# Folding the last three pieces of the first transform stage to sum and difference, with its stores on another queue and one weight load moved back

## The chip, the cores and the metric

The kernel runs on one core of one Trainium2 chip. The metric is the device time of one execution in microseconds, as the median of several runs; lower is better. The engines named below are TensorE (PE in the profile), VectorE (DVE), ScalarE (ACT), GpSimd (POOL) and SyncE (SP). SP only issues DMA transfers here; ACT and POOL can issue them as well.

## The reference, cut to what matters

```python
X = np.fft.fft(x, axis=1)          # x: (8, 3136, 256) float32
X = np.fft.fft(X, axis=2)
x = X.real
mu, var = mean and variance of x over the last axis
xn = (x - mu) / np.sqrt(var + 1e-06) * g_ln
return x + np.maximum(xn @ w_ch1, 0.0) @ w_ch2     # w_ch1: 256x1024, w_ch2: 1024x256
```

A real part of a two-dimensional FFT for each of eight batches, then a layer norm and a two-layer MLP with a residual.

## The kernel before, in words

The transform along the sequence (3136 = 64 x 49) goes in two steps. **Step 1** is a 64-point transform for each of 49 residues; it is done in seven *pieces* (`i` = 0..6), each with its own load of 512 KB (`load_x(b, i)`, tile `xs`). Its result goes through `store1` to a DRAM scratch and comes back in another layout through `relayout` (tile `s2`). **Step 2** (`step2`) sums over the 49 residues, and its PSUM result is split into a high and a low part (`ckh`, `ckl`) that the MLP's matmuls read. The main loop then runs the MLP (`moe1_a`, `moe1_b`, `moe2`) over chunks of 256 rows, with the later batches' steps 1 and 2 placed between its matmuls.

Before the loop stands a head, written out by hand, of some 40 us. It does three things at once: step 1 of batch 0 from the seven loads of `x`; the conversion of the first weight matrix, given as float64, to two fp32 parts; and the same for the second matrix. The first matrix comes in four quarters of 512 KB (`load_w1(0..3)`, called w1_0 to w1_3 here). For each quarter ACT computes `ew` (`convert_z`), and DVE the rest: `mw` and `fw` (`convert_m`), two operations on `ew` (`convert_b`) and the scaled quarter `gw` (`finish_w1`). PE then multiplies two quarters at a time with a table (`transform_w1`, tile `psw`), ACT rounds the result (`round_w1`, `w_hi`), and a remainder is formed (`rest_w1`, `w_lo`). The second matrix's first two quarters (`load_w2(0)`, `load_w2(1)`, called w2_0 and w2_1) are loaded into the places of w1_0 and w1_1, so each waits until those have been read.

In step 1 the channels are folded first: `fold_zw` makes two 256-column tiles z and w of a piece. For batch 0, PE then forms the sum part and the difference part by accumulating in PSUM: four fp32 matmuls of 256 columns per piece, z and w with one table for the sum half, z and w with the table and its negative for the other half. The later batches form the sum and the difference on POOL (`fold_eo`) and use split operands. Two channels (0 and 128) go apart, through `ends` on POOL and `step1_ends` on PE and ACT.

The order on PE, ACT, DVE and POOL is the order in which the program is written (`manual_schedule`), as is SP's in the head. DMAs that SP and ACT issue take eight completion semaphores in turn, `DMAHW0` to `DMAHW7`; one that reuses a semaphore first waits, on its issuing engine, until the transfer that had it before has landed.

The lines that matter in the profile of before: L255 and L257 are step 1's matmuls, L265 the copy of a piece out of PSUM, L269 `store1`, L276 `relayout`, L309 step 2's matmuls, L330 and L334 `ckh` and `ckl`, L520 to L535 and L563 the conversion on DVE, L528 its ACT part, L549 and L554 the weight loads, L573 `transform_w1`, L679 `warm_up` (bf16 matmuls on zeros between the weight transforms and step 2).

Of the kernel before, what the change touches and what calls it, by code (L numbers as in the profile page):

```python
# [25 lines left out]
ALU = mybir.AluOpType  # L26
# [120 lines left out]
def tile_kernel(ctx: ExitStack, tc: tile.TileContext, x, g_ln, w1, w2, tu, tab, tz, ty, tw, out):  # L147
    nc = tc.nc
# [30 lines left out]
    def load_x(b, i):  # L179
        in_order(nc.sync.dma_start(xs[:, i], x[b, i]))  # L180
# [26 lines left out]
        eng.tensor_tensor(out=z, in0=a[:, :, 1:129], in1=c[:, :, 255:127:-1], op=ALU.add)  # L207
        eng.tensor_tensor(out=w, in0=a[:, :, 255:127:-1], in1=c[:, :, 1:129], op=ALU.add)

    def fold_eo(b, i):  # L210
        z, w = zw.pop((b, i))
        f = work.tile([128, 2, 2, 128], F32, tag="fold", name=f"f{b}_{i}")
        nc.gpsimd.tensor_tensor(out=f[:, :, 0], in0=z, in1=w, op=ALU.add)
        nc.gpsimd.tensor_tensor(out=f[:, :, 1], in0=z, in1=w, op=ALU.subtract)
        pieces[b, i] = [f]

    def fold_hi(b, i):
# [29 lines left out]
    def step1(b, i):  # L247
        alloc1(b)
        ps = psum.tile([128, 2, 2, 128], F32, tag="y" if b else f"acc{i % 2}", name=f"ps1_{b}_{i}",
                       bufs=1 if b else 2)  # L250
        if b == 0:
            z, w = zw.pop((b, i))
            for h in range(2):
                o = ps[:, :, h]
                nc.tensor.matmul(o, tu_s[:, 0:128], z, start=(h == 0), stop=False,  # L255
                                 skip_group_check=True)
                nc.tensor.matmul(o, tu_s[:, 128 * h:128 * h + 128], w, start=False, stop=True,  # L257
                                 skip_group_check=True)
        else:
            p = pieces.pop((b, i))  # L260
            for n, (ti, xi) in enumerate(PASSES):
                nc.tensor.matmul(ps, (t1_hi, t1_lo)[ti], p[xi],  # L262
                                 start=(n == 0), stop=(n == 2))
        s = s1[b][:, 2 * i:2 * i + 2]
        nc.scalar.copy(s[:, :, :, :127], ps[:, :, :, :127])  # L265
# [13 lines left out]
    gb = group_bounds()  # L279
# [266 lines left out]
    def load_w1(n):  # L546
        wp = w1p_all[:, 4 * n:4 * n + 4].rearrange("p a d -> p (a d)").bitcast(I64)
        i, k = n % 2, n // 2
        nc.sync.dma_start(wp, w1[128 * i:128 * i + 128, 512 * k:512 * k + 512])  # L549
        w1p.append(wp)  # L550

    def load_w2(n):
        wp = w1p[n]
        nc.sync.dma_start(wp.rearrange("p (f d) -> p f d", f=2), w2v[:, 2 * n:2 * n + 2])  # L554
        w2p.append(wp)
# [126 lines left out]
    with tc.manual_schedule(engines={E.PE, E.Activation, E.DVE, E.Pool}):  # L682
        with tc.manual_schedule(engines={E.SP}):
            nc.vector.memset(one, 1.0)
            for t in (warm, warm_h):
                nc.vector.memset(t, 0.0)
            for n, t in ((3, warm), (5, warm_h)):
                warm_up(n, t)
            nc.scalar.dma_start(g_s, g_ln.rearrange("(i p) -> p i", p=128))
            nc.scalar.activation(one, one, AF.Sqrt)  # L690
            nc.sync.dma_start(tu_s, tu)
            load_x(0, 0)
            load_x(0, 1)
            load_w1(0)
            for i in (2, 3, 4):
                load_x(0, i)
            load_w1(1)
            for i in (5, 6):
                load_x(0, i)
            load_w1(2)  # L700
            load_w1(3)
            nc.sync.dma_start(tw_all, tw)
            nc.gpsimd.memset(zmu, 0.0)
            nc.gpsimd.memset(masked, 0.0)
            ends(0, 0, 6)
            fold_zw(0, 0, nc.vector)
            step1(0, 0)
            nc.vector.tensor_scalar_mul(g_s, g_s, 2.0 ** -20)
            fold_zw(0, 1, nc.vector)
            convert_z("w1_0", w1p[0])  # L710
            step1(0, 1)
            convert_m("w1_0", w1p[0])
            fold_zw(0, 2, nc.vector)
            step1(0, 2)
            convert_b("w1_0")
            load_w2(0)
            nc.sync.dma_start(tab_s[:, :, :gb[4]], tab[:, :, :gb[4]])
            nc.sync.dma_start(tz_s, tz)
            step1_ends(0, 0, 6)
            for i in range(3):  # L720
                store1(0, i, nc.scalar if i % 2 else nc.gpsimd)
            ends(0, 6, 10)
            fold_zw(0, 3, nc.vector)
            step1(0, 3)
            convert_z("w1_1", w1p[1])
            fold_zw(0, 4, nc.vector)
            step1(0, 4)
            finish_w1(0)
            step1_ends(0, 6, 10)
            store1(0, 3, nc.scalar)  # L730
            store1(0, 4, nc.gpsimd)
            ends(0, 10, NS)
            convert_m("w1_1", w1p[1])
            fold_zw(0, 5, nc.vector)
            step1(0, 5)
            convert_z("w1_2", w1p[2])
            convert_b("w1_1")
            load_w2(1)
            fold_zw(0, 6, nc.vector)
            step1_ends(0, 10, NS)  # L740
            store1(0, 5, nc.scalar)
            step1(0, 6)
            store1(0, 6, nc.gpsimd)
            finish_w1(1)
            convert_z("w1_3", w1p[3])
            convert_m("w1_2", w1p[2])
            convert_b("w1_2")
            finish_w1(2)
            relayout(0, 0, 4)
            relayout(0, 4, 8)  # L750
            load_w2(2)
            nc.sync.dma_start(tab_s[:, :, gb[4]:gb[8]], tab[:, :, gb[4]:gb[8]])
            relayout(0, 8, 16)
            nc.scalar.copy(minus, tw_all[:, 512:])
            transform_w1(0, 0)
            transform_w1(0, 1)
            round_w1(0)
            convert_m("w1_3", w1p[3])
            convert_b("w1_3")
            load_w2(3)  # L760
            nc.sync.dma_start(ty_s, ty)
            nc.sync.dma_start(tab_s[:, :, gb[8]:], tab[:, :, gb[8]:])
            for i in range(NU):
                load_x(1, i)
            finish_w1(3)
            transform_w1(1, 0)
            rest_w1(0)
            convert_z("w2_0", w2p[0])
            convert_z("w2_1", w2p[1])
            rest_w1_copy(0)  # L770
            transform_w1(1, 1)
            round_w1(1)
            convert_m("w2_0", w2p[0])
            convert_b("w2_0")
            f = finish_w2(0)
            split_w2(0, f)
            convert_m("w2_1", w2p[1])
            convert_b("w2_1")
            warm_up(15, warm_h)
            step2(0, "m")  # L780
            step2(0, "hl")
            step2(1, "m")
            step2(1, "hl", 0)
            f = finish_w2(1)
            moe1_a(0, ((1, 0), (0, 0), (0, 1)))
            split_w2(1, f)
            step2(0, "f")
            moe1_a(1, ((1, 0), (0, 0), (0, 1)))
            rest_w1(1)
            moe1_b(0)  # L790
            moe1_a(2)
            moe1_b(1)
            moe1_b(2)
            moe1_a(3)
            rest_w1_copy(1)
            step2(1, "f")
            convert_a("w2_2", w2p[2])
            step2(1, "hl", 1)
            moe2(0)
            moe1_b(3)  # L800
            moe1_a(4)
            convert_b("w2_2")
            f = finish_w2(2)
            nc.gpsimd.tensor_scalar(out=neg, in0=ty_s[:, 1, 129:130], scalar1=2.0, scalar2=-1.0,
                                    op0=ALU.mult, op1=ALU.add)
            moe2(1)
            step2(2, "m")
            moe1_b(4)
            split_w2(2, f)
            moe1_a(5)  # L810
            step2(2, "hf")
            step2(2, "l")
            convert_a("w2_3", w2p[3])
            moe2(2)
            add_late(6, convert_b, "w2_3")
            add_late(6, lambda: w2f.append(finish_w2(3)))
            add_late(7, lambda: split_w2(3, w2f.pop()))
            add_late(14, split, t1_hi, t1_lo, tu_s[:, 0:128])

        main.append(True)  # L820
        lag, last = 3, 8 * NCH
        for s in range(6, last):
            moe1_b(s - 1)
            moe1_a(s)
            for fn, args in late.get(s, ()):
                fn(*args)
            moe2(s - lag)
            for fn, args in after.get(s, ()):
                fn(*args)
        moe1_b(last - 1)  # L830
        inverse_std(LC)
        moe2(last - 3)
        for i, side in ((0, 0), (1, 0), (0, 1), (1, 1)):
            for t in (last - 2, last - 1):
                moe2(t, ((i, side),))
            finish_last(i, side)
# [18 lines left out]
```

## Time and profile before

| | |
|---|---|
| median of 3 runs | 999.56 us (999.49 to 1001.34) |
| profiled execution, its own time | 1001.5 us |
| its span, first to last instruction | 999.7 us |
| PE busy | 988.3 us (99%) |
| DVE, ACT, POOL busy | 817.8, 534.8, 248.3 us |
| granted TensorE clock | 1.000 |

The profiled execution took 1.8 us more than its span. PE is busy nearly all the time; the one place where it is not is the head, where the first of the page's forty slices (25 us each) shows DVE at 6 tenths and POOL at 1. All that the change touches lies in the first 37 us.

### The profile page before, as it was taken

The page shows a single profiled execution, that of the slowest core. Times are in us where ns is not written, and L with a number is a line of the kernel's source. Part 1 is how long each engine was busy: PE and PEld are TensorE (multiplying, and loading weights), DVE is VectorE, ACT ScalarE, POOL GpSimd, SP SyncE. Part 2 cuts the span into 40 slices and gives each one's busy share as a digit, 9 for nine tenths or more (in the row PEclk, how much of TensorE's full clock was granted, in tenths as well). Part 3 has the DMA queues.
Part 4 walks back from the last instruction along what each step waited for, and adds up shares of the span by engine and source line. Part 5 has one row for each costly group of instructions (what it writes and reads, how often), then busy time and mean ns, then how long its engine had stood idle before and what let it go on. Part 6 is the DMA issues. An engine that isn't in the chain of part 4 may idle for free.

```text
span 999.7 us, 21759 instructions
## 1 busy us (share of the span) xinstructions
PE 988.3 (99%) x8288; PEld 966.4 (97%) x8289; DVE 817.8 (82%) x2190; ACT 534.8 (53%) x1416; POOL 248.3 (25%) x278
## 2 busy tenths in 40 slices
PE   9999999999999999999999999999999999999998
PEld 6799999999999999999999999999999999999998
DVE  6788878788888888888887888888888888787887
ACT  3555555555555555555555556555555555554553
POOL 1145434212411432232342124113322300000000
PEclk9999999999999999999999999999999999999999
DMA  9943352124222242121521242212310112100101
GB/s 342 264 151 113 121 159 85 64 75 132 91 73 76 75 133 99 66 75 64 170 85 54 85 134 89 95 54 71 111 53 35 54 52 87 43 23 22 44 22 43
DMA packets 41528, 92.10 MB, mean 92 GB/s; under 512 B 4176, under 2 KB 18704, under 8 KB 40528
## 3 DMA queue, kind: packets, MB, share of 16 engines
q1 hardware_dynamic: 40016, 88.87, 27.1%
q8 instruction: 66, 1.08, 0.5%
q0 software_dynamic: 320, 1.05, 0.3%
q10 hardware_dynamic: 1088, 0.79, 0.2%
q14 instruction: 38, 0.31, 0.1%
HBM read 50.32 MB, written 40.37 MB: 91 GB/s over the span
## 4 chain that ended last, share of the span: by engine, by line
PE 88%; DVE 7%; ACT 2%; DMA 1%; issue 1%; ACTq 0%; SPq 0%; DVEq 0%
PE acc L404 49%; PE ab L354 24%; PE ps L309 5%; PE psy L428 4%; PE ps L262 3%; DVE h_lo L369 2%; DVE h L360 1%; DVE h L361 1%; ACT h_hi L368 1%; PE pw L679 1%; PE ps L255 1%; DMA scratch<-s 1%; PE ps L257 1%; DMA s<-scratch 1%; DVE st L450 0%
## 5 line engine op out<-in xcount | busy, mean ns | idle before, releaser
L404 PE MATMUL acc<-w_hi,h_lo 128*128 128x256 f32 x1568 | 435.2, 278 | 0.2 <-DVE h_lo L369 0.2
L404 PE MATMUL acc<-w_lo,h_hi 128*128 128x256 f32 x1568 | 435.0, 277 | 0.0
L404 PE MATMUL acc<-w_hi,h_hi 128*128 128x256 f32 x1568 | 435.0, 277 | 0.0
L369 DVE SCALAR_TENSOR_TENSOR h_lo<-h,h_hi 128x512 fp32r<-128x512 f32 x392 | 295.5, 754 | 148.7 <-ACT h_hi L368 146.6
L368 ACT ACTIVATE h_hi<-h 128x512 fp32r<-128x512 f32 x392 | 249.9, 638 | 296.6 <-DVE h L361 296.4
L404 PEld LDWEIGHTS acc<-w_hi,h_hi 128*128 128x128 f32 x1568 | 295.6, 189 | 0.0
L404 PEld LDWEIGHTS acc<-w_hi,h_lo 128*128 128x128 f32 x1568 | 294.6, 188 | 0.5 <-DVE h_lo L369 0.4
L404 PEld LDWEIGHTS acc<-w_lo,h_hi 128*128 128x128 f32 x1568 | 294.7, 188 | 0.0
L354 PE MATMUL ab<-ckl,w_hi 128*128 128x256 f32 x768 | 218.8, 285 | 2.2 <-DVE h L361 2.1
L354 PE MATMUL ab<-ckh,w_lo 128*128 128x256 f32 x768 | 213.6, 278 | 0.5 <-ACT ckh L330 0.3
L354 PE MATMUL ab<-ckh,w_hi 128*128 128x256 f32 x768 | 213.1, 277 | 0.0
L225 POOL TENSOR_TENSOR fl<-f,fh 128x512 fp32r<-128x512 f32 x49 | 64.0, 1307 | 513.1 <-ACT fh L219 475.7
L360 DVE TENSOR_TENSOR h<-asb,ab 128x256 f32<-128x256 f32 x384 | 158.7, 413 | 1.6 <-ACT asb L359 1.5
L361 DVE TENSOR_TENSOR h<-asb,ab 128x256 f32<-128x256 f32 x384 | 158.9, 414 | 0.0
L354 PEld LDWEIGHTS ab<-ckl,w_hi 128*128 128x128 f32 x768 | 144.3, 188 | 5.9 <-issue 1.7
L354 PEld LDWEIGHTS ab<-ckh,w_lo 128*128 128x128 f32 x768 | 144.4, 188 | 3.1 <-ACT ckh L330 0.5
L354 PEld LDWEIGHTS ab<-ckh,w_hi 128*128 128x128 f32 x768 | 144.8, 189 | 0.0
L359 ACT COPY asb<-ab 128x256 f32<-128x256 f32 x384 | 138.1, 360 | 11.6 <-PE ab L354 9.7
L265 ACT COPY s<-ps 128x508 f32<-128x508 f32 x56 | 32.7, 584 | 67.0 <-PE ps L262 53.3
L309 PE MATMUL ps<-tab_s,s 112*128 112x98 f32 (+1 forms) x512 | 65.5, 273 | 1.1 <-DMA s<-scratch 1.1
L309 PEld LDWEIGHTS ps<-tab_s,s 112*128 112x128 f32 x512 | 61.8, 191 | 1.6 <-issue 1.6
L330 ACT CAST ckh<-ps 128x392 fp32r<-128x392 f32 (+49 forms) x112 | 39.8, 356 | 43.0 <-PE ps L309 42.8
(108 smaller groups left out, 965.5 us busy)
## 6 DMA issues: line engine op xcount, KB each, us to landing
xs<-x SPq DMA_DIRECT2D x56, 512.0 KB, 3.9
out<-o SPq DMA_DIRECT2D x96, 256.0 KB, 2.0
scratch<-s SPq DMA_DIRECT2D x49, 256.0 KB, 2.3
s<-scratch SPq DMA_DIRECT2D x7, 1792.0 KB, 10.0
w1p_all<-w SPq DMA_DIRECT2D x8, 512.0 KB, 8.6
scratch<-s POOLq DMA_DIRECT2D x4, 256.0 KB, 6.0
s<-scratch SPq DMA_DIRECT2D x2, 448.0 KB, 5.9
s<-scratch SPq DMA_DIRECT2D x1, 896.0 KB, 12.1
```

Source lines behind the costliest of these rows:

```text
L225: nc.gpsimd.tensor_tensor(out=lo, in0=f, in1=hi.bitcast(F32), op=ALU.subtract)
L265: nc.scalar.copy(s[:, :, :, :127], ps[:, :, :, :127])
L309: nc.tensor.matmul(ps[:, h, k0 - base:k1 - base], s2[b][:KP, g, 128 * h:128 * h + 128], tab_s[:, h, k0:k1], start=(h == 0 and g == 2 * j), ...
L330: nc.scalar.copy(hi, src)
L354: nc.tensor.matmul(pt, wt[wi][:, j, fs], ch[xi][:, j, :w], start=(n == 0), stop=(n == 2))
L359: nc.scalar.copy(asb[:, :w], pa)
L360: nc.vector.tensor_tensor(out=h[:, :w], in0=asb[:, :w], in1=pb, op=ALU.add)
L361: nc.vector.tensor_tensor(out=h[:, w:], in0=asb[:, :m], in1=pb[:, :m], op=ALU.subtract)
L368: nc.scalar.activation(h_hi, h, AF.Relu)
L369: nc.vector.scalar_tensor_tensor(out=h_lo, in0=h, scalar=0.0, in1=h_hi.bitcast(F32), op0=ALU.max, op1=ALU.subtract)
L404: nc.tensor.matmul(acc[c, i][:, side], hs[xi][:, h0:h0 + 128], ws[wi][:, f], start=(f == 0 and side == 0 and n == 0), stop=(f == 7 and n = ...
L428: nc.tensor.matmul(ps[:, j, :129 + j], ck[:, j], ty_s[:, j, :129 + j], start=(j == 0), stop=True, skip_group_check=True)
```

## The change: what it does

For pieces 4, 5 and 6 of batch 0, the sum and the difference are made ahead of PE by `fold_eo`, for piece 4 on POOL and for pieces 5 and 6 on DVE, into one tile of 512 columns, and PE does one fp32 matmul of 512 columns with the table in place of four of 256. All seven stores of batch 0 go through ACT's queue; before, four of them (pieces 0, 2, 4, 6) were issued by POOL. The load of w1_1 moves behind the seven loads of `x`, and the table `tw` ahead of w1_2. The conversion of w1_0 is finished later, and all of the conversions of w1_1, w1_2 and w1_3 stand behind the last store. The load of w2_1 moves behind the first `relayout`, and the first part of the table `tab` and `tz` behind the last store.

```diff
-    def fold_eo(b, i):
+    def fold_eo(b, i, eng=nc.gpsimd):
         z, w = zw.pop((b, i))
         f = work.tile([128, 2, 2, 128], F32, tag="fold", name=f"f{b}_{i}")
-        nc.gpsimd.tensor_tensor(out=f[:, :, 0], in0=z, in1=w, op=ALU.add)
-        nc.gpsimd.tensor_tensor(out=f[:, :, 1], in0=z, in1=w, op=ALU.subtract)
+        eng.tensor_tensor(out=f[:, :, 0], in0=z, in1=w, op=ALU.add)
+        eng.tensor_tensor(out=f[:, :, 1], in0=z, in1=w, op=ALU.subtract)
...
-        if b == 0:
+        if (b, i) in zw:
             z, w = zw.pop((b, i))
...
+        elif b == 0:
+            nc.tensor.matmul(ps, tu_s[:, 0:128], pieces.pop((b, i))[0], start=True, stop=True)
...
             for i in (2, 3, 4):
                 load_x(0, i)
-            load_w1(1)
             for i in (5, 6):
                 load_x(0, i)
+            load_w1(1)
+            nc.sync.dma_start(tw_all, tw)
             load_w1(2)
             load_w1(3)
-            nc.sync.dma_start(tw_all, tw)
...
             for i in range(3):
-                store1(0, i, nc.scalar if i % 2 else nc.gpsimd)
+                store1(0, i, nc.scalar)
...
             fold_zw(0, 5, nc.vector)
+            fold_eo(0, 5, nc.vector)
             step1(0, 5)
-            convert_z("w1_2", w1p[2])
-            convert_b("w1_1")
-            load_w2(1)
             fold_zw(0, 6, nc.vector)
+            fold_eo(0, 6, nc.vector)
             step1_ends(0, 10, NS)
             store1(0, 5, nc.scalar)
             step1(0, 6)
-            store1(0, 6, nc.gpsimd)
+            store1(0, 6, nc.scalar)
+            finish_w1(0)
+            nc.sync.dma_start(tab_s[:, :, :gb[4]], tab[:, :, :gb[4]])
+            nc.sync.dma_start(tz_s, tz)
+            convert_z("w1_1", w1p[1])
+            convert_m("w1_1", w1p[1])
+            convert_b("w1_1")
             finish_w1(1)
+            convert_z("w1_2", w1p[2])
...
             relayout(0, 0, 4)
+            load_w2(1)
             relayout(0, 4, 8)
```

ACT's queue before, from the copy of piece 4 to the table's cast (`s` is step 1's result, `pse` the two channels that go apart; what a row waits for stands in brackets):

```order
L265 COPY s_0_135<-ps_0_4_195 128x4x127 [waits PE_49]
L243 COPY s_0_135<-pse_0_203 128x8 [waits PE_49]
L269 DMA scratch_136<-s_0_135 128x2x256 [waits DMAHW5_49,Activation_49]
L265 COPY s_0_135<-ps_0_5_218 128x4x127 [waits PE_49]
L528 ACTIVATE ew_2_224<-w1p_all 128x512 [waits DMAHW4_49]
L243 COPY s_0_135<-pse_0_232 128x8 [waits PE_49]
L245 COPY zmu<-pse_0_232 112x1 [waits Pool_49]
L269 DMA scratch_136<-s_0_135 128x2x256 [waits Activation_49]
L265 COPY s_0_135<-ps_0_6_239 128x4x127 [waits PE_49]
L528 ACTIVATE ew_3_248<-w1p_all 128x512 [waits DMAHW6_49]
```

The same place after the change:

```order
L267 COPY s_0_135<-ps_0_4_199 128x4x127 [waits PE_49]
L271 DMA scratch_136<-s_0_135 128x2x256 [waits DMAHW1_49,Activation_49]
L267 COPY s_0_135<-ps_0_5_211 128x4x127 [waits PE_49]
L243 COPY s_0_135<-pse_0_220 128x8 [waits PE_49]
L245 COPY zmu<-pse_0_220 112x1 [waits Pool_49]
L271 DMA scratch_136<-s_0_135 128x2x256 [waits DMAHW3_49,Activation_49]
L267 COPY s_0_135<-ps_0_6_227 128x4x127 [waits PE_49]
L271 DMA scratch_136<-s_0_135 128x2x256 [waits DMAHW5_49,Activation_49]
L530 ACTIVATE ew_1_235<-w1p_all 128x512 [waits DMAHW4_49]
L530 ACTIVATE ew_2_245<-w1p_all 128x512 [waits DMAHW0_49]
L530 ACTIVATE ew_3_247<-w1p_all 128x512 [waits DMAHW2_49]
```

The `ew` rows of w1_1, w1_2 and w1_3 now stand behind the last store. Counted through the list of DMAs, the semaphore `DMAHW3` that the store of piece 5 waits for was last used by the store of piece 1, and `DMAHW5`, for which the store of piece 6 waits, by the store of piece 2.

DVE's queue before, from piece 3 to piece 6 (`zw` is `fold_zw`, L563 `finish_w1`):

```order
L207 TENSOR_TENSOR zw_3_181<-xs 128x256 [waits DMAHW6_49,PE_49]
L208 TENSOR_TENSOR zw_3_181<-xs 128x256
L207 TENSOR_TENSOR zw_4_192<-xs 128x256 [waits DMAHW7_49]
L208 TENSOR_TENSOR zw_4_192<-xs 128x256
L563 SCALAR_TENSOR_TENSOR gw_201<-fw_0_156,g_s,ew_0_147 128x2x256 [waits DVE_49]
L520 TENSOR_SCALAR mw_1_211<-w1p_all 128x512 [waits DMAHW0_49]
L522 SCALAR_TENSOR_TENSOR fw_1_212<-w1p_all,mw_1_211 128x512 [waits DVE_49]
L207 TENSOR_TENSOR zw_5_215<-xs 128x256 [waits DMAHW1_49]
L208 TENSOR_TENSOR zw_5_215<-xs 128x256
L533 TENSOR_SCALAR ew_1_190<-ew_1_190 128x512 [waits Activation_49]
L535 SCALAR_TENSOR_TENSOR ew_1_190<-w1p_all,ew_1_190 128x512 [waits DVE_49]
```

And after the change, from piece 5 on:

```order
L207 TENSOR_TENSOR zw_5_205<-xs 128x256 [waits DMAHW0_49]
L208 TENSOR_TENSOR zw_5_205<-xs 128x256
L213 TENSOR_TENSOR f_5_208<-zw_5_205 128x2x128 [waits DVE_49]
L214 TENSOR_TENSOR f_5_208<-zw_5_205 128x2x128
L207 TENSOR_TENSOR zw_6_214<-xs 128x256 [waits DMAHW1_49]
L208 TENSOR_TENSOR zw_6_214<-xs 128x256
L213 TENSOR_TENSOR f_6_217<-zw_6_214 128x2x128 [waits DVE_49,PE_49]
L214 TENSOR_TENSOR f_6_217<-zw_6_214 128x2x128
L565 SCALAR_TENSOR_TENSOR gw_231<-fw_0_156,g_s,ew_0_147 128x2x256
L522 TENSOR_SCALAR mw_1_237<-w1p_all 128x512 [waits DMAHW4_49]
L524 SCALAR_TENSOR_TENSOR fw_1_238<-w1p_all,mw_1_237 128x512 [waits DVE_49]
L535 TENSOR_SCALAR ew_1_235<-ew_1_235 128x512 [waits Activation_49]
```

Four operations of `fold_eo` (L213, L214) are new on DVE, and the whole conversion of three quarters of the first matrix now follows piece 6; before, w1_1's stood between pieces 4 and 6.

More of the change, by code (lines that the diff above doesn't have):

```diff
@@ L714, in tile_kernel @@
             step1(0, 2)
[L715 to L718, printed above, removed]
             step1_ends(0, 0, 6)
             for i in range(3):
-                store1(0, i, nc.scalar if i % 2 else nc.gpsimd)
+                store1(0, i, nc.scalar)
             ends(0, 6, 10)
@@ L724, in tile_kernel @@
             step1(0, 3)
-            convert_z("w1_1", w1p[1])
             fold_zw(0, 4, nc.vector)
-            step1(0, 4)
-            finish_w1(0)
+            fold_eo(0, 4)
+            convert_b("w1_0")
+            load_w2(0)
             step1_ends(0, 6, 10)
             store1(0, 3, nc.scalar)
-            store1(0, 4, nc.gpsimd)
+            step1(0, 4)
+            store1(0, 4, nc.scalar)
             ends(0, 10, NS)
-            convert_m("w1_1", w1p[1])
             fold_zw(0, 5, nc.vector)
+            fold_eo(0, 5, nc.vector)
             step1(0, 5)
-            convert_z("w1_2", w1p[2])
-            convert_b("w1_1")
-            load_w2(1)
             fold_zw(0, 6, nc.vector)
+            fold_eo(0, 6, nc.vector)
             step1_ends(0, 10, NS)
```

## The prediction

> **What bounds the kernel now.** The page comes first. PE is the bound of the whole, so a change in the head pays one for one only if the moment moves at which PE begins its steady work.
>
> ```profile
> PE 988.3 (99%) x8288; PEld 966.4 (97%) x8289; DVE 817.8 (82%) x2190; ACT 534.8 (53%) x1416; POOL 248.3 (25%) x278
> ```
>
> Then the chain of waits of the first 37 us, in order of time (start, us, what). It tells what sets that moment.
>
> ```profile
> 15.02 0.43 PE ps L257 x2
> ...
> 20.09 0.54 PE ps L255 x2
> 20.62 0.43 PE ps L257 x2
> 21.06 0.43 PE ps L255 x2
> 21.49 0.45 PE ps L257 x2
> ...
> 21.96 0.59 ACT s L265
> ...
> 22.84 5.30 DMA scratch<-s
> ...
> 28.35 5.25 DMA s<-scratch
> ...
> 33.73 0.66 PE ps L309 x4
> ...
> 35.99 0.27 ACT ckh L330
> ...
> 36.30 0.70 PE ab L354 x3
> ```
>
> The chain is step 1 on PE until 21.93, the copy of piece 6, its store (5.30 us), the relayout (5.25 us), step 2 at 33.73, the MLP at 36.30. The first row closes piece 3 at 15.45; piece 6 alone is the four rows from 20.09, 1.85 us. Beside this chain runs the conversion of the weights, which the chain does not show because it ends earlier. PE's timeline has its end:
>
> ```profile
> 1.50 5.31 PE L679 MATMUL pw<-warm 128*128 128x512 f32 x6 [1.50 <-DVE warm L686]
> ...
> 21.78 5.42 PE L573 MATMUL psw<-gw,tw_all 128*128 128x512 f32 x12
> ...
> 27.50 1.88 PE L573 MATMUL psw<-gw,tw_all 128*128 128x512 f32 x4
> 29.43 3.19 PE L679 MATMUL pw<-warm_h 128*128 128x512 bf16 x14
> ```
>
> An fp32 matmul shows as two records, so the 12 records of L573 are six matmuls of 512 columns, 0.90 us each. The last two of `transform_w1` (1.88 us) and `warm_up` (3.19 us) end at 32.6, so the weight path is only 1.1 us ahead of the relayout. That 1.1 us is all the cover it has.
>
> **Part 1: fold and fewer matmuls.** A piece of 1.85 us becomes one matmul of 0.90 us. Three pieces save 3 x 0.95 = 2.85 us, and step 1 would end on PE at 21.93 - 2.85 = 19.1. Whether the operands are there depends on loads, DVE and POOL. For the loads I show two issues from SP's timeline, each followed by its time to landing from the DMA view of that moment:
>
> ```profile
> 7.28 0.33 SPq L180 DMA_DIRECT2D xs<-x  x1
> xs<-x SPq DMA_DIRECT2D x1, 512.0 KB, 9.2
> 8.84 0.33 SPq L549 DMA_DIRECT2D w1p_all<-w  x1
> w1p_all<-w SPq DMA_DIRECT2D x1, 512.0 KB, 8.9
> ```
>
> Piece 6's x lands at 16.5, w1_2 at 17.7: 512 KB take about 1.28 us in a full queue. With w1_1 taken out from among them, the x of pieces 5 and 6 land 1.28 us earlier, at 13.9 and 15.2; piece 4's, ahead of w1_1, stays at 16.5 - 3 x 1.28 = 12.6. DVE and POOL give the folds:
>
> ```profile
> 17.75 0.42 DVE L207 TENSOR_TENSOR zw<-xs 128x256 f32<-128x256 f32 x1
> 18.08 0.42 DVE L208 TENSOR_TENSOR zw<-xs 128x256 f32<-128x256 f32 x1
> ...
> 22.44 0.42 DVE L520 TENSOR_SCALAR mw<-w1p_all 128x512 int32<-128x512 int32 x1
> ...
> 23.50 0.42 DVE L533 TENSOR_SCALAR ew<-ew 128x512 int32<-128x512 int32 x1
> ...
> 24.68 0.75 DVE L563 SCALAR_TENSOR_TENSOR gw<-fw,g_s,ew 128x512 f32<-128x512 f32 x1
> 25.35 0.42 DVE L520 TENSOR_SCALAR mw<-w1p_all 128x512 int32<-128x512 int32 x1
> ...
> 60.76 0.73 POOL L213 TENSOR_TENSOR f<-zw 128x256 f32<-128x256 f32 x1
> ...
> 69.48 1.19 POOL L214 TENSOR_TENSOR f<-zw 128x256 f32<-128x256 f32 x1
> ```
>
> A DVE operation of this size follows the next at 0.33 us. Piece 4 on DVE ends near 13.4, POOL needs 2 x 0.73 to 2 x 1.19 us, so it has the fold between 14.9 and 15.8; PE wants it at 15.45 plus the short matmuls of the two channels, about 15.8. Cost 0, by that cover. Then DVE finishes w1_0's two operations on `ew` (1.2 us), z, w and the two fold operations of piece 5 (1.35 us, to 15.9) and of piece 6 (piece 6's fold reuses piece 4's tile, free at 16.7), so the last fold is ready at 17.3; PE wants it at 19.1 - 0.9 = 18.2. The cover is 0.9 us. Step 1 ends at 19.1, and ACT's copy (0.59 us) at 19.7.
>
> **Part 2: the stores on ACT's queue.** The price of an issue falls out of the path, but a wait comes with it: the store of piece 5 waits until that of piece 1 has landed, the store of piece 6 for that of piece 2. ACT stands still meanwhile, and behind these two stand the copy of piece 6 and the `ew` of three quarters. When do the early stores land? Rows: the first store that ACT issues and its time to landing; what the SP queue (q1) moved from 14 to 17 us, in packets, MB and share of the engines; what ACT's queue (q10) moved from 23 to 24 us; the later stores in a quiet stretch, from the page; and SP's longest wait.
>
> ```profile
> 14.02 0.37 ACTq L269 DMA_DIRECT2D scratch<-s  x1
> scratch<-s ACTq DMA_DIRECT2D x1, 256.0 KB, 8.2
> q1 hardware_dynamic: 342, 1.23, 102.4%
> q10 hardware_dynamic: 288, 0.28, 78.6%
> scratch<-s SPq DMA_DIRECT2D x49, 256.0 KB, 2.3
> SPq L717 <- DMA scratch<-s: 6.6, 1, 6.6
> ```
>
> From 14 to 17 us SP's queue alone moved, although a store had been issued at 14.02, and that store took 8.2 us; SP's load of `tab` waited 6.6 us for it, the same kind of wait that ACT gets now. After the change SP's queue holds, at 14.0, piece 6's x, w1_1, `tw` and w1_2, by the 1.28 us spacing work until about 17.3. From there the three stores (0.79 MB) go at between 0.28 and 0.36 MB/us (0.28 over its share of 0.786), 2.5 us, and land 2.3 - 0.26/0.28 = 1.4 us after their last byte: the store of piece 2 at 21.2. So I take 21.2 for ACT's last store. Bounds: 19.7 if the waits cost nothing (the copy of piece 6 is ready then); 23.0 if the third store, issued at 14.02 + 2 x 0.37 = 14.8, takes 8.2 us as the measured one. The truth should be between, since w1_3 and `tab` no longer run among them.
>
> **Part 3: the conversions behind the stores.** `ew` of w1_1 is ready 0.37 us and about 0.6 us (its rows in part 4 read 0.68 and overlap the next operation) after the last store begins, at 22.2. DVE did its first two operations on that quarter meanwhile. From the rows above, `ew`'s two operations and `gw` take 25.35 - 23.50 = 1.85 us and a whole quarter 25.35 - 22.44 = 2.91 us: 22.2 + 1.85 + 2 x 2.91 = 29.9 for the last `gw`. PE then does the last pair (1.88) and `warm_up` (3.19) and can begin step 2 at 35.0 instead of 33.73. Bounds from the two values of part 2: 33.4 and 36.8. The load of w1_3 now waits for the store of piece 0 (about 19.5), and DVE wants it at 22.2 + 1.85 + 2.91 = 27.0. In a full queue (8.9 us) it would come at 28.4, 1.4 us late; behind an empty one, as here, by the 5.7 us row shown in part 4, at 25.2. I take the second and cost 0.
>
> **Part 4: w2_1 behind the first relayout.** ACT's order has `ew` of w2_1 ahead of `ckh`, with these rows, the first of them waiting for w2_1's landing:
>
> ```profile
> 29.46 0.68 ACT L528 ACTIVATE ew<-w1p_all 128x512 f32<-128x512 f32 x1 [2.79 <-DMA w1p_all<-w]
> ...
> 31.95 0.64 ACT L539 CAST w_hi<-fw 128x512 fp32r<-128x512 f32 x1
> ...
> 35.10 0.48 ACT L330 CAST ckh<-ps 128x390 fp32r<-128x390 f32 x1 [2.51 <-PE ps L309]
> ```
>
> From landing to readiness for `ckh` are 31.95 + 0.64 - 29.46 = 3.1 us, and ACT then idled 2.51 us. Now w2_1 is issued right behind the relayout, so 0.7 us after the last store landed. That store lands between 21.2 + 2.3 = 23.5 (quiet) and 28.1 (as now); the same bytes stand ahead of it as now except w2_1's 1.28 us, so I take 26.3, near the upper end. The time to landing of w2_1 is bounded by two rows, its own and that of the weight load that stood behind two relayouts:
>
> ```profile
> w1p_all<-w SPq DMA_DIRECT2D x1, 512.0 KB, 5.7
> w1p_all<-w SPq DMA_DIRECT2D x1, 512.0 KB, 7.9
> ```
>
> Behind one relayout I take 6.3: 26.3 + 0.7 + 6.3 = 33.3, and `ckh` can run at 36.4 instead of 35.10, +1.3. The bounds give 33.0 and 39.8. The relayout itself, 26.5 + 5.25 = 31.8, is no longer last.
>
> **The sum.** Step 1 is 2.85 us shorter and the relayout lands about 1.8 us earlier, but step 2 waits for the weight path (+1.3) and `ckh` for the later of that (35.0 + 35.10 - 33.73 = 36.4) and of w2_1 (36.4). Both come out at +1.3 us. On the profiled execution: span 999.7 to 1001.0, time 1001.5 to 1002.8; its time stands 1.9 us over the median of the runs, so on the median 999.56 + 1.3 = 1000.9. From 0.2% on, 2.0 us, a measurement of this kernel can tell a difference; this is less.
>
> **Rivals.**
> *The stores stay slow.* If the store of piece 2 lands as the measured one did, ACT is free at 23.0 and step 2 begins at 36.8, +3.1: 1002.6. For it speaks the 8.2 us row; against it, that w1_3 and `tw` with w2_0 behind were on the queue then. It passes 2.0 us from a last store at 21.9 on.
> *The relayout stays the bound and is earlier.* Should the conversions not be last, the full 2.85 us come off: 996.7. For this ACT would have to have `ew` of w1_1 by 17.3 + 0.67 + 1.06 = 19.0, ahead of the copy of piece 6; then the last `gw` is at 17.3 + 0.67 + 3 x 2.91 = 26.7 and step 2 at 31.8, -1.9: 997.6. The order puts `ew` behind the last store, so -0.3 (step 2 at 33.4) is the floor by my rows, 999.3. Only a mistake in them gives more.
> *The clock falls.* PE would be without work for up to 2 us between transforms. The first row of PE's timeline shows fp32 matmuls at 5.31/6 = 0.89 us a record against 5.42/12 = 0.45 later, so a PE that had been idle runs at half speed although the granted clock reads 1.0. If that came back ahead of the last pair, 1.88 and 3.19 us would double, +5.1 on top: 1006.0. For it speaks that PE's work there is spread over 10 us with gaps; against it, that a 1.1 us gap before step 2 now costs nothing. [...]
>
> **How the numbers follow.** Forecast, from -0.5 to +2.0 us: 62%. Slow stores (or w2_1 late), +2.0 to +3.5: 20%. The faster case: 13%, of it 8% beyond 2.0 us. The clock: 5%, more than 2 us slower. Faster by over 0.2%: 0.08; within: 0.67 (62 and 5 of the faster case); slower: 0.25. The range leaves out the clock, the fuller gain and the worst of the slow stores: 998.4 to 1003.0. It takes in the two bounds of step 2 (-0.3 and +3.1) and a spread of runs of about 1 us below. The likeliest case's own range is 999.1 to 1001.6.
>
> **What would show it.** Right: 128x512 matmuls in step 1 with PE's end near 19.1; ACT idle before its last two stores, released by a store's landing; `ew` of w1_1 near 21.6; a last `gw` near 30; `warm_up` right ahead of step 2 with no wait for the relayout between. Wrong: step 2 again waiting for the relayout (parts 2 and 3 too dear), PE waiting for a fold (part 1), a weight load arriving after 27 us, or `warm_up` records longer than 0.23 us (the clock).

## The result, and the profile after

The changed kernel is slower: 1004.55 us median of 9 runs (1001.61 to 1008.0) against 999.91 us (9 runs) for the kernel before, a ratio of 1.0043 with a 95% interval of 1.0029 to 1.0056. That is under half a per cent, but clear of the spread of the runs. The prediction said 1000.9 us, in a range from 998.4 to 1003.0. The profiled execution has a span of 1003.8 us, 4.1 us more than that of before.

PE's share on the page shows that no steady work was added; PE is as busy as it was, for a longer span.

```profile
PE 988.0 (98%) x8270; PEld 964.6 (96%) x8271; DVE 820.3 (82%) x2194; ACT 535.4 (53%) x1416; POOL 246.9 (25%) x276
```

PE's timeline of after (start, us, what, and in brackets the idle time before it). L260 is the new matmul of 512 columns, L575 `transform_w1`, L681 `warm_up`, L311 step 2, L356 the MLP's first matmuls, L406 its second ones (tile `acc`):

```profile
15.35 1.13 PE L260 MATMUL ps<-f,tu_s 128*128 128x512 f32 x2
16.78 1.12 PE L260 MATMUL ps<-f,tu_s 128*128 128x512 f32 x2 [0.31 <-DVE f L214]
...
18.32 1.12 PE L260 MATMUL ps<-f,tu_s 128*128 128x512 f32 x2
...
23.88 1.98 PE L575 MATMUL psw<-gw,tw_all 128*128 128x512 f32 x4 [1.97 <-DVE gw L565]
...
29.70 1.98 PE L575 MATMUL psw<-gw,tw_all 128*128 128x512 f32 x4 [0.47 <-DVE gw L565]
31.74 3.19 PE L681 MATMUL pw<-warm_h 128*128 128x512 bf16 x14
34.98 0.69 PE L311 MATMUL ps<-tab_s,s 112*128 112x99 f32 x4
...
39.92 0.58 PE L356 MATMUL ab<-ckh,w_lo 128*128 128x256 f32 x1 [2.68 <-ACT ckh L332]
...
45.17 0.28 PE L406 MATMUL acc<-w_hi,h_lo 128*128 128x256 f32 x1
```

Step 1 ends at about 19.3 instead of 21.9. Step 2 begins at 34.98, against 33.73, right behind `warm_up`: the weight path sets it, not the relayout. Then comes what is new: 2.68 us without work, until `ckh` is there, and an MLP that begins at 39.92 against 36.30.

The chain of waits of after says what `ckh` was late for:

```profile
20.76 0.37 ACTq L271
...
21.17 0.69 ACT ew L530
...
28.17 0.70 DVE ew L537
...
28.95 7.14 DMA w1p_all<-w
...
36.17 0.69 ACT ew L530
36.86 0.96 ACT w_lo L593 x2
37.82 0.98 ACT w_hi L583 x2
38.80 0.52 ACT w_hi L541
39.32 0.56 ACT ckh L332 x2
...
39.92 1.87 PE ab L356 x6
```

The load of w2_1 is issued at 28.95 and lands at 36.09. ACT's `ew` of that quarter stands ahead of `ckh` in ACT's order, with 3.1 us of work between landing and `ckh`. (The chain goes from DVE's `ew` at 28.17 to the load's issue because the two came at nearly the same time. What held the load was SP's order: it stands behind the relayout, whose wait for the store is shown below. What the load needs itself, the place of w1_1, was free by 23.06, when experiment 1 issued it.) ACT's timeline has the wait at the last two stores, one for w1_3, and the long one for w2_1:

```profile
19.74 0.37 ACTq L271 DMA_DIRECT2D scratch<-s  x1
20.15 0.58 ACT L267 COPY s<-ps 128x508 f32<-128x508 f32 x1 [1.44 <-DMA scratch<-s]
20.76 0.37 ACTq L271 DMA_DIRECT2D scratch<-s  x1
...
24.76 0.68 ACT L530 ACTIVATE ew<-w1p_all 128x512 f32<-128x512 f32 x1 [2.35 <-DMA w1p_all<-w]
...
36.17 0.69 ACT L530 ACTIVATE ew<-w1p_all 128x512 f32<-128x512 f32 x1 [8.99 <-DMA w1p_all<-w]
...
39.17 0.70 ACT L332 CAST ckh<-ps 128x390 fp32r<-128x390 f32 x2
```

SP issued the first relayout and, behind it, w2_1 only when the stores had landed. The DMA view gives the time to landing of the last store (issued 20.76) and of w2_1:

```profile
scratch<-s ACTq DMA_DIRECT2D x1, 256.0 KB, 7.7
w1p_all<-w SPq DMA_DIRECT2D x1, 512.0 KB, 7.1
```

SP's waits (total, times, longest) have the relayout's for the store, and that of w1_3's load (L551) for the store of piece 0:

```profile
SPq L278 <- DMA scratch<-s: 6.8, 2, 5.8
SPq L551 <- DMA scratch<-s: 5.0, 1, 5.0
```

So the last store landed at 28.45, although it was issued 20.76; before, the last store landed at 28.1. The 2.6 us that step 1 had gained were gone at this point. The DMA view of the stretches 22 to 23 and 25 to 26 us shows where the store was: in the first SP's queue (q1) alone moved, in the second both (packets, MB, share).

```profile
q1 hardware_dynamic: 52, 0.18, 78.0%
...
q1 hardware_dynamic: 147, 0.23, 61.2%
q10 hardware_dynamic: 166, 0.16, 45.9%
```

Last, the granted clock (the column before the DMA share) in the two 0.2 us stretches in which it changed; all between them read 0.50:

```profile
39.60:39.80 0.20, 0.00 (x0) 0.00 (x0) 0.07 (x1) 0.20 (x2) 0.20 (x1) 0.70 0.74 180
43.00:43.20 0.20, 0.20 (x3) 0.16 (x1) 0.00 (x0) 0.20 (x2) 0.20 (x1) 0.77 0.94 210
```

From 39.7 to 43.1 PE ran at half speed. From the MLP's first matmul to the first one of `acc` (L404 before, L406 after) it took 5.25 us (39.92 to 45.17) against 4.43 before (36.30 to 40.73; the row of before):

```profile
40.73 0.28 PE L404 MATMUL acc<-w_hi,h_lo 128*128 128x256 f32 x1
```

So at the first `acc` the profiled execution is 4.44 us late, in three parts: step 2 later by 1.25; the MLP's start later against step 2 by 2.37 (4.94 us behind it, before 2.57), which is w2_1; and 0.82 at half speed.

### The profile page after: what moved, and what is told of

The parts are those of the page before. It is cut to its first block, busy times and chain, and to the rows that moved or that the text cites. A ratio compares the mean times of both kernels' runs of the same rounds, so it can differ in the third digit from the quotient of the medians.

```text
span 1003.8 us, 21727 instructions
## 1 busy us (share of the span) xinstructions
PE 988.0 (98%) x8270; PEld 964.6 (96%) x8271; DVE 820.3 (82%) x2194; ACT 535.4 (53%) x1416; POOL 246.9 (25%) x276
## 4 chain that ended last, share of the span: by engine, by line
PE 87%; DVE 7%; ACT 3%; DMA 2%; issue 1%; ACTq 0%; DVEq 0%; SPq 0%
PE acc L406 48%; PE ab L356 24%; PE ps L311 5%; PE psy L430 4%; PE ps L264 3%; DVE h_lo L371 2%; DVE h L362 1%; DVE h L363 1%; DMA scratch<-s 1%; ACT h_hi L370 1%; DMA w1p_all<-w 1%; PE pw L681 1%; DVE st L452 0%; DVE ew L537 0%; ACT asb L361 0%
## 5 line engine op out<-in xcount | busy, mean ns | idle before, releaser
L406 PE MATMUL acc<-w_hi,h_lo 128*128 128x256 f32 x1568 | 435.3, 278 | 0.1
L406 PE MATMUL acc<-w_hi,h_hi 128*128 128x256 f32 x1568 | 435.1, 277 | 0.0
L406 PE MATMUL acc<-w_lo,h_hi 128*128 128x256 f32 x1568 | 435.1, 277 | 0.0
L406 PEld LDWEIGHTS acc<-w_hi,h_hi 128*128 128x128 f32 x1568 | 295.6, 189 | 0.0
L406 PEld LDWEIGHTS acc<-w_hi,h_lo 128*128 128x128 f32 x1568 | 294.5, 188 | 0.5 <-DVE h_lo L371 0.3
L406 PEld LDWEIGHTS acc<-w_lo,h_hi 128*128 128x128 f32 x1568 | 294.7, 188 | 0.0
L356 PE MATMUL ab<-ckl,w_hi 128*128 128x256 f32 x768 | 219.5, 286 | 1.5 <-DVE h L363 1.4
L356 PE MATMUL ab<-ckh,w_lo 128*128 128x256 f32 x768 | 214.2, 279 | 2.9 <-ACT ckh L332 2.7
L356 PE MATMUL ab<-ckh,w_hi 128*128 128x256 f32 x768 | 213.7, 278 | 0.0
L356 PEld LDWEIGHTS ab<-ckh,w_lo 128*128 128x128 f32 x768 | 145.0, 189 | 5.6 <-ACT ckh L332 2.8
L356 PEld LDWEIGHTS ab<-ckl,w_hi 128*128 128x128 f32 x768 | 144.8, 189 | 5.0 <-issue 1.7
L356 PEld LDWEIGHTS ab<-ckh,w_hi 128*128 128x128 f32 x768 | 145.4, 189 | 0.0
L311 PE MATMUL ps<-tab_s,s 112*128 112x98 f32 (+1 forms) x512 | 65.6, 273 | 0.1
L311 PEld LDWEIGHTS ps<-tab_s,s 112*128 112x128 f32 x512 | 61.8, 191 | 0.6 <-PE pw L681 0.6
L332 ACT CAST ckh<-ps 128x392 fp32r<-128x392 f32 (+49 forms) x112 | 39.7, 357 | 40.1 <-PE ps L311 39.9
```

Of the source, the lines that this page charges most:

```text
L311: nc.tensor.matmul(ps[:, h, k0 - base:k1 - base], s2[b][:KP, g, 128 * h:128 * h + 128], tab_s[:, h, k0:k1], start=(h == 0 and g == 2 * j), ...
L332: nc.scalar.copy(hi, src)
L356: nc.tensor.matmul(pt, wt[wi][:, j, fs], ch[xi][:, j, :w], start=(n == 0), stop=(n == 2))
L406: nc.tensor.matmul(acc[c, i][:, side], hs[xi][:, h0:h0 + 128], ws[wi][:, f], start=(f == 0 and side == 0 and n == 0), stop=(f == 7 and n = ...
```

## The experiments

Theory A throughout: the load of w2_1 behind the relayout holds ACT and so the MLP (the larger part), the conversions behind the stores hold step 2 (the smaller), the fold and the stores' queue cost nothing by themselves. The rivals are in the expectations. Ratios are to the kernel before, on the same chip. "Kernel 7" below is the kernel of experiment 7, and so on.

**1. The changed kernel with w2_1 ahead of the relayout.**

```diff
+            load_w2(1)
             relayout(0, 0, 4)
-            load_w2(1)
             relayout(0, 4, 8)
```

> The changed kernel with one line moved: the load of w2_1 stands ahead of the first relayout again (behind tab and tz). Theory A (the landing of w2_1, issued behind the relayout, holds ACT and so the first MLP matmul): w2_1 lands near 30 instead of 36.1, ckh runs as soon as step 2 has results, step 2 still begins near 35.0 behind the weight path, the MLP near 37.4 instead of 39.9: 2.5 to 3 us less than the changed kernel, about 1001.5, 1.3 us over the kernel before. Theory B (the late stores and the relayout are what holds it, 28.5 for the last store against 28.1): nothing gained, 1004 to 1005. Theory C (half-speed PE behind its gap is the price): at most 1.3 us gained, if the gap closes.

Measured: 1001.74 us, ratio 1.0011 (1.0002 to 1.0020). PE's timeline of this run:

```profile
23.83 5.40 PE L575 MATMUL psw<-gw,tw_all 128*128 128x512 f32 x8 [1.96 <-DVE gw L565]
...
34.94 0.69 PE L311 MATMUL ps<-tab_s,s 112*128 112x99 f32 x4
...
37.54 0.38 PE L356 MATMUL ab<-ckh,w_lo 128*128 128x256 f32 x1 [0.35 <-ACT ckh L332]
```

And ACT's:

```profile
36.33 0.48 ACT L332 CAST ckh<-ps 128x390 fp32r<-128x390 f32 x1 [3.17 <-PE ps L311]
```

`ckh` now waits for step 2's PE work, as before the change; the MLP begins at 37.54, +1.24. The load of w2_1 was issued at 23.06. Step 2's start has not moved (34.94). Taking this one line back takes 3.2 of the 4.3 us (0.0032 of the ratio) away. PE's first row shows a half-speed stretch that costs nothing up to step 2, which begins when it did after the change: 8 records in 5.40 us, 0.68 each against 0.50 in the 1.98 us of four at the same place after the change; DVE's `gw` sets the pace there.

**2. The fold alone, on the kernel before.** The diff's three `fold_eo` calls and its matmul, each call right behind its `fold_zw`; stores and loads as before.

> The kernel before with the fold alone: pieces 4, 5 and 6 of batch 0 folded by POOL (4) and DVE (5, 6), one matmul each; stores, loads and conversions in their old places. Theory A: the fold is not what costs; DVE has 1.36 us more ahead of the conversions, PE's step 1 ends 0.5 to 1 us earlier since DVE is late, and step 2 begins between 33.2 and 34.2: within 0.5 us of the kernel before. A rival (the four more DVE operations push the whole weight path): +1.0 to +1.4 us.

Measured: 1002.12 us, 1.0012 (1.0003 to 1.0021), a loss. PE's timeline:

```profile
17.26 1.13 PE L260 MATMUL ps<-f,tu_s 128*128 128x512 f32 x2 [2.54 <-POOL f L214]
...
18.59 1.99 PE L260 MATMUL ps<-f,tu_s 128*128 128x512 f32 x2
```

The loss is of the size that the rival gave, but not by its mechanism: the fold on POOL stood behind POOL's two store issues (1.62 us at 13.55), so PE waited 2.54 us for it and then ran at half speed (1.99 us for the next piece's matmul instead of 1.13). Moving the stores to ACT is what makes room for the fold on POOL.

**3. The stores alone, on the kernel before.**

```diff
-                store1(0, i, nc.scalar if i % 2 else nc.gpsimd)
+                store1(0, i, nc.scalar)
...
-            store1(0, 4, nc.gpsimd)
+            store1(0, 4, nc.scalar)
...
-            store1(0, 6, nc.gpsimd)
+            store1(0, 6, nc.scalar)
```

> The kernel before with all seven stores of batch 0 in ACT's queue, nothing else. The semaphores of the DMAs are dealt out anew by this, so w1_3 and tw wait for other transfers than before. Theory A: ACT waits at its last stores, ew of w1_3 comes later and the last store lands 0 to 1.5 us later than 28.1; +0 to +1.5 us. Theory B (the queue of the stores is the whole loss of 4.3 us): +3 to +4.5 us. If the queue makes the stores faster: the last lands by 27 and the time falls by about 1 us.

Measured: 1000.99 us, 1.0003 (0.9994 to 1.0012): no difference that can be told. Step 2 began at 34.03 in the profiled execution, the MLP at 36.63.

**4. The changed kernel with a longer `warm_up`.** `warm_up(22, warm_h)` in place of 15; it puts PE's work right up to the time at which `ckh` can run.

> The changed kernel with warm_up of 22 in place of 15 matmuls ahead of step 2, so that PE's gap ahead of the MLP (2.7 us, behind which it ran at a granted clock of 0.5 for 3.5 us) shrinks to about 1 us. Theory A (w2_1 holds the start): PE runs the first MLP matmuls at full clock, but ACT and DVE set the pace there, so 0 to 0.8 us less than the changed kernel. Theory C (the clock is the larger part of the 4 us): 1.3 to 2.5 us less, and a smaller spread of the runs.

Measured: 1003.65 us, 1.0034 (1.0022 to 1.0047). The clock read 1.00 at the MLP, which began at 39.07 with `acc` at 43.70, 4.63 us later. Part of the earlier start is not the filling: ACT had w2_1 at 35.27 here, 0.9 us earlier than in the profiled execution of the changed kernel. The time is 0.9 us under the changed kernel's by the ratios, but the intervals overlap.

**5. The changed kernel with w2_0 and the tables behind the first relayout**, a single run: is it these loads, issued by SP just ahead of the last stores, that hold the stores back?

```diff
-            load_w2(0)
...
-            nc.sync.dma_start(tab_s[:, :, :gb[4]], tab[:, :, :gb[4]])
-            nc.sync.dma_start(tz_s, tz)
...
             relayout(0, 0, 4)
+            load_w2(0)
+            nc.sync.dma_start(tab_s[:, :, :gb[4]], tab[:, :, :gb[4]])
+            nc.sync.dma_start(tz_s, tz)
             load_w2(1)
```

> The changed kernel with the loads of w2_0, of the first part of tab and of tz behind the first relayout too, to see what holds the last two stores. They were issued at 19.7 and 20.8 us in the changed kernel and moved nothing until 24, while w1_3, w2_0 and tab, issued at 19.0 to 20.6, moved. Theory A (the transfers issued just ahead hold them): with only w1_3 ahead the last store lands by 25.5 instead of 28.5. Theory B (stores in ACT's queue are slow by themselves): 28 as before. The time is no test here: w2_0, tab and w2_1 come later, so step 2 and the MLP begin later than in the changed kernel or about as late.

Measured: 1004.77 us once, span 1003.0. The DMA view at the last store's issue:

```profile
scratch<-s ACTq DMA_DIRECT2D x1, 256.0 KB, 4.7
```

ACT's timeline, at `ew` of w2_0 and of w2_1:

```profile
33.16 0.69 ACT L530 ACTIVATE ew<-w1p_all 128x512 f32<-128x512 f32 x1 [5.14 <-DMA w1p_all<-w]
36.65 0.69 ACT L530 ACTIVATE ew<-w1p_all 128x512 f32<-128x512 f32 x1 [2.81 <-DMA w1p_all<-w]
```

The store, issued at 20.95, landed in 4.7 us in place of 7.7, in this one execution: it is the loads issued ahead of it that hold it. The time did not improve, because two quarters of the second matrix now come late, and ACT meets the second of them at 36.65.

**6. Kernel 1 (experiment 1's) with `ew` of w1_1 and w1_2 ahead of the last two stores.**

```diff
             store1(0, 4, nc.scalar)
+            convert_z("w1_1", w1p[1])
...
+            convert_z("w1_2", w1p[2])
             store1(0, 5, nc.scalar)
...
-            convert_z("w1_1", w1p[1])
...
-            convert_z("w1_2", w1p[2])
```

> The kernel with w2_1 ahead of the relayout again, and with ACT's ew of w1_1 and w1_2 ahead of the last two stores; by this order the store of piece 5 no longer waits for an earlier store's landing and that of piece 6 for another one. Theory A (with w2_1 ahead, the remaining 1.1 us over the kernel before come from ew behind the waiting stores): the last gw at 27.0 to 28.0 instead of 29.6, warm_up's end at 32 to 33, step 2 at 32.3 to 33.8: -1.4 to +0.3 us against the kernel before. If the relayout becomes last again, step 2 begins 5 us behind the last store's landing. Theory B (the remainder is the clock or the DMA total): still +1 us, step 2 near 35.

Measured: 1000.05 us, 0.9995 (0.9986 to 1.0003), span 998.4. PE's timeline:

```profile
27.82 1.98 PE L575 MATMUL psw<-gw,tw_all 128*128 128x512 f32 x4 [0.47 <-DVE gw L565]
29.86 3.19 PE L681 MATMUL pw<-warm_h 128*128 128x512 bf16 x14
33.10 0.69 PE L311 MATMUL ps<-tab_s,s 112*128 112x99 f32 x4
...
35.70 0.39 PE L356 MATMUL ab<-ckh,w_lo 128*128 128x256 f32 x1 [0.35 <-ACT ckh L332]
```

The weight path is 1.9 us shorter than after the change, and the loss is gone. This is the best version run, with the fold and the stores on ACT kept; it is level with the kernel before and not shown to be faster.

**7. Only w2_1 moved, on the kernel before.** The same line as in experiment 1, moved the other way.

> The kernel before with one line moved: the load of w2_1 behind the first relayout, as in the changed kernel. Theory A (this line is the larger part of the loss): w2_1 issued near 28.5, landing 7 us later near 35.5, ckh 3.1 us behind that near 38.7, the MLP near 39.4 instead of 36.3: +3 us, 1.003, and PE at a lower clock after its gap in some runs. Theory B (the loss belongs to the stores and conversions together): less than +1 us.

Measured: 1004.16 us, 1.0036 (1.0022 to 1.0050): this one line reproduces nearly all of the loss. The time is theory A's, but the rows are not: the MLP was to begin near 39.4, and began at 37.72. ACT's timeline:

```profile
33.97 0.69 ACT L528 ACTIVATE ew<-w1p_all 128x512 f32<-128x512 f32 x1 [7.29 <-DMA w1p_all<-w]
```

PE's:

```profile
37.72 0.58 PE L354 MATMUL ab<-ckh,w_lo 128*128 128x256 f32 x1 [2.78 <-ACT ckh L330]
```

The two 0.2 us stretches in which the granted clock changed:

```profile
36.80:37.00 0.20, 0.00 (x0) 0.00 (x0) 0.00 (x0) 0.20 (x2) 0.00 (x0) 0.61 1.07 268
43.60:43.80 0.20, 0.20 (x4) 0.20 (x3) 0.20 (x1) 0.20 (x1) 0.00 (x0) 0.82 1.17 298
```

The MLP starts 1.42 us late, and half speed from 36.9 to 43.7 adds 1.74 to the first `acc` (6.17 us behind the start, before 4.43).

**8. Only w1_1 moved behind x, on the kernel before.** `load_w1(1)` stands ahead of `load_w1(2)`.

> The kernel before with the load of w1_1 behind the seven loads of x, nothing else. The x of pieces 5 and 6 land 1.3 us earlier, w1_1 2.5 us later (near 16.5), while DVE's conversion of it still stands ahead of piece 5, so DVE waits 1 to 2 us there. Theory A: pieces 5 and 6 come 1 to 2 us later out of DVE and PE, and the last store with them: +0.5 to +2 us. A rival (x earlier is a gain by itself): -0.5 to -1 us.

Measured: 1001.80 us, 1.0013 (1.0003 to 1.0024). PE's timeline:

```profile
18.01 0.70 PE L255 MATMUL ps<-zw,tu_s 128*128 128x256 f32 x2 [0.98 <-DVE zw L207]
...
34.84 0.66 PE L309 MATMUL ps<-tab_s,s 112*128 112x99 f32 x4 [1.82 <-DMA s<-scratch]
```

A small loss: PE waits for DVE, which in this order has w1_1's operations ahead of a fold, and the relayout is later. The profiled execution, 1003.85 us, is one of the longer ones: its granted clock also read 0.50 from 36.2 to 43.05. In the changed kernel the load's place is not the loss by itself, since experiment 6 has it there too.

**9 and 10. Is the clock part of the time?** Eleven bf16 matmuls on zeros between step 2 and the MLP, in the changed kernel and in kernel 7.

```diff
             step2(1, "hl", 0)
+            warm_up(11, warm_h, "ab", 2)
             f = finish_w2(1)
```

> The changed kernel with 11 bf16 matmuls on zeros (0.228 us each, 2.5 us, by the 14 of 3.19 us in its trace) put on PE between step 2's last matmul and the MLP's first, into the PSUM buffer that the MLP's second matmul group will use. Nothing else moves: the MLP still begins at 39.9, when `ckh` is there. Theory A (part of the loss is the clock that falls to 0.50 after PE's 2.68 us without work): the granted clock reads 1.00 from 39 to 44, the MLP's first matmuls are 0.115 us apart and not 0.21, the first `acc` matmul comes at 39.92 + 4.43 = 44.35 as the 4.43 us of the kernel before have it, not at 45.17, and the time is 0.8 us below the changed kernel's, 1.0035 of before. Rival (the clock's rows cost nothing, since DVE and ACT set the MLP's first steps and PE catches up): `acc` at 45.2 and the time as the changed kernel's, 1.0043. A second rival: the half clock returns later all the same, and the gain is under 0.4 us.

> The kernel before with only the load of w2_1 moved behind the first relayout, and with the same 11 bf16 matmuls between step 2 and the MLP. Without them the MLP began at 37.72 (+1.42), the first `acc` matmul at 43.89 (+3.16) with a granted clock of 0.50 from 37 to 43.6, and the time was 1.0036 of before. Theory A (the +1.42 is the wait for the load, the other 1.7 us are the clock): clock 1.00 throughout, `acc` at 37.72 + 4.43 = 42.15, time 1.0014 to 1.0018 of before. Rival (the load's place costs more than the later start, by what it does to the relayouts and the loads behind it): `acc` stays above 43.2 at full clock and the time above 1.0028.

Measured: the changed kernel so filled 1004.17 us, 1.0031 (1.0020 to 1.0042); kernel 7 so filled 1003.65 us, 1.0024 (1.0015 to 1.0033). From 36 to 44 us the clock read 1.00 in both profiled executions. PE's timeline of the first:

```profile
37.50 2.54 PE L681 MATMUL pw<-warm_h 128*128 128x512 bf16 x11
39.69 0.47 PE L356 MATMUL ab<-ckh,w_lo 128*128 128x256 f32 x1
```

ACT's:

```profile
33.85 0.70 ACT L530 ACTIVATE ew<-w1p_all 128x512 f32<-128x512 f32 x1 [6.36 <-DMA w1p_all<-w]
...
37.70 0.26 ACT L332 CAST ckh<-ps 128x122 fp32r<-128x122 f32 x1 [0.33 <-PE ps L311]
```

From the MLP's start to `acc` it now takes 4.40 us (39.69 to 44.09), as theory A has it. But w2_1 happened to land at 33.8 here, 2.3 us earlier than in the profiled execution of the changed kernel, and the filling itself then held the MLP: `ckh` was there at 37.96. In kernel 10 the reverse happened: the relayout was issued at 29.28, in kernel 7 at 28.09, with nothing changed ahead of it, and the MLP began at 39.46 in place of 37.72; then `acc` came 4.72 us later in place of 6.17. So the rows show what half speed costs in an execution, 0.8 us for the shorter stretch and about 1.5 to 1.7 for the longer. By the times it is not shown: the ratios of 4, 9 and 10 lie 0.0009 to 0.0012 under their unfilled versions, with intervals that overlap, and kernel 10 missed theory A's 1.0018; its `acc`, 44.18, came where the rival had it (above 43.2).

The other runs have a granted clock too, as a mean over the whole execution; one stretch of 3.4 us at half speed takes 0.0017 off it, two take 0.0034. All nine runs of the changed kernel and all five of kernel 7 read 0.996 to 0.998, so each had some half speed in it. The kernel before, measured beside the experiments, read 1.000 in 51 of 69 runs and 0.998 in 13, and on each of the three chips the 13 are on the mean 0.8 to 1.6 us longer. Five of the seven runs of kernel 9 and ten of the eleven of kernel 10 read 1.000, and on the mean these still take 3.6 and 2.9 us more than the kernel before's runs at 1.000 on that chip (1004.15 and 1003.42 against 1000.56). So most of the loss is there at full clock, though in kernel 9 the filling itself held the MLP. How much of kernel 7's median is clock and how much later landings stays open.

## Why the prediction was wrong

*Part 1, the fold: right.* Step 1 ended on PE at about 19.3 (predicted 19.1), with a wait of 0.31 us for a fold that was to cost nothing. That it bought nothing was in the sum too; experiment 2 adds that it needs the stores moved off POOL, since there PE waited 2.54 us for the fold behind them.

*Part 2, the stores on ACT: right in its time, half right in its way.* ACT's last store went out at 20.76 (21.2). Only the store of piece 5 waited for a landing (the 1.44 us ahead of the copy at 20.15); that of piece 6, which was to wait for the store of piece 2, went out as soon as its copy was done.

*Part 3, the conversions behind the stores: right.* The last `gw` ended at 29.65 (29.9), w1_3 was there at 24.74 (25.2), step 2 began at 34.98 (35.0). Experiment 6 shows the cause by taking it away: with two `ew` ahead of the stores step 2 began at 33.10.

*Part 4, w2_1 behind the relayout: the step that failed, by size.* `ckh` was to run at 36.4 and ran at 39.17. The term that was mis-sized most is the landing of the last store, 26.3 in the prediction and 28.45 measured, a little outside its bound of 28.1. The other versions of this order bear it out: their first relayouts were issued, once the store was there, at 29.13, 29.07 and 27.90 (experiments 1, with w2_1 ahead of it, 4 and 9). The prediction argued that "the same bytes stand ahead of it as now except w2_1's". The bytes were the same, but not their time: w1_3 was held on SP until the store of piece 0 had landed (5.0 us at L551), and w2_0 behind it; they went out at 19.04 and 19.50, `tab` at 19.92, all within 1.8 us of the last store. Experiment 5 shows it, in one execution: without w2_0 and the tables there, the store took 4.7 us. The second part is w2_1's own time, 7.1 us for 6.3 predicted; it varies (5.4 in experiments 7 and 9). Behind these, the 3.1 us from landing to `ckh` held to the tenth (36.17 to 39.32).

*The clock: a rival with the right effect in the wrong place.* It had 5%, ahead of the last pair of `transform_w1`, at +5.1 us. It came behind step 2, because part 4's error opened a gap of 2.68 us there, and its price to the first `acc` was 0.8. The gaps at which the clock went to 0.50 were of 2.68, 2.78, 2.54, 1.96 and 1.82 us (after, experiments 7, 2, 1 and 8); in the first two it fell before the gap was over, in the others 0.2 to 1.4 us behind it. Among the transforms, where the rival looked for it, it fell in experiments 1 and 5 (24.0 to 27.4 and 24.5 to 27.9), ahead of the last pair and over before it; step 2 began at 34.94 and 35.16, against 34.98 after the change, so nothing like +5.1 us came of it.

*The sum and the range.* The sum was +1.3 us. With the measured terms in part 4's places, 28.45 + 0.5 + 7.14 + 3.1 = 39.2 for `ckh`; its two casts (0.70 us together) lie between that and the MLP, at 39.9: +3.6 on 36.30. The clock adds 0.8, which makes the +4.4 at the first `acc`. The bound that the prediction itself had worked out for `ckh`, 39.8 (+4.7), covered this but for the clock. The range took in the bounds of step 2 (up to +3.1) and not this one: "w2_1 late" stood with the slow stores in a rival that ended at +3.5.

## What to carry to other kernels

When a load is moved behind something that waits, price it from the landing of what it now waits for, and ask when the transfers ahead of that will be issued, not only whether their bytes are the same. Then follow the in-order engine that consumes the load: here one line cost 3 us because ACT's work on weights that were needed only later stood ahead of the cast that PE needed at once. A bound that has been worked out belongs in the range, above all where the quantity (a landing) varies by 1 to 2 us between executions of one order (here w2_1 took 7.1 us in the changed kernel and 5.4 in experiment 9, and the first relayout went out at 28.09 in kernel 7 and at 29.28 in kernel 10).

## What the runs showed of the hardware

Half speed came in stretches of one length or twice that: 39.7 to 43.1 in the changed kernel and 24.0 to 27.4 in experiment 1 (3.4 us each), 36.9 to 43.7 in experiment 7 (6.8 us). Experiment 5 has two stretches in one execution, and they begin 17.1 us apart (24.5 and 41.6), about five times 3.4. The length of a gap alone does not tell whether the clock falls: the gap of 1.96 us ahead of 23.83 in experiment 1 was followed by it, and the gap of 1.97 us ahead of 23.88 in the changed kernel, at the same place, was not (four records in 1.98 us); nor was one of 1.80 us in experiment 3, ahead of 23.14.

PE's work ahead of a fall was little: ahead of the seven falls in the heads (after the change, experiments 1, 2, 7 and 8, and two in 5) PE was busy for 0.95 to 1.59 us of the 3.4 us that end where the clock falls. That alone does not tell either: of the 3.4 us that end at 23.88 in the changed kernel PE was busy for 1.13 us, and the clock read 1.00 there and up to 27. What makes the clock fall, and why half speed lasts 3.4 or 6.8 us, no run shows.

The last two stores, issued on ACT's queue at 19.74 and 20.76, moved next to nothing until 24 (23 packets on that queue from 21 to 22, none from 22 to 23, 3 from 23 to 24; by 24 it had moved 1.32 MB in all, which is five stores of 256 KB), while SP's queue, with three loads issued from 19.04 to 19.92, moved alone; from 22 to 23 the engines were not all busy (78%). Once the stores moved, both queues moved about equal numbers of packets (147 and 166 from 25 to 26). Why the stores moved next to nothing before that, no run here tells.
